# Grouped-query attention with a key/value cache: keys in rows of 32 KiB, two units to a K buffer, two V buffers

## The chip, the core and the metric

One core of a Trainium2 chip runs the kernel. The metric is the device time in microseconds (us), the median of the runs. The engines are named as in the profile: PE (matrix products; PEld its weight loads), DVE (vector), ACT (scalar), POOL (GpSimd) and SP, whose queue issues all of this kernel's transfers. Each engine takes its instructions in the order in which the program names them, and waits at one for the semaphores of its inputs and of the buffer that it writes.

## What is computed

```python
B, Sq, D = 8, 4, 512
Hq, Hkv, Sk, Dh = 32, 8, 2048, 128
rep = Hq // Hkv
q = (x @ wq).reshape(B, Sq, Hq, Dh).transpose(0, 2, 1, 3)
k = jnp.repeat(k_cache, rep, axis=1)
v = jnp.repeat(v_cache, rep, axis=1)
scores = jnp.einsum("bhqd,bhkd->bhqk", q, k) * (Dh ** -0.5)
p = softmax(scores, axis=-1)
o = jnp.einsum("bhqk,bhkd->bhqd", p, v)
out = o.transpose(0, 2, 1, 3).reshape(B, Sq, Hq * Dh) @ wo
```

All arrays are bf16. k_cache and v_cache have 33.6 MB each, wq and wo 4.2 MB each, x 32 KB.

## The kernel before

The work is cut into 16 **units**: a unit is one batch entry with four of the eight key heads (units 0 to 7 have heads 0 to 3, units 8 to 15 heads 4 to 7). Its K is 2 MB and its V is 2 MB. In memory the four heads of a batch entry lie one behind the other, so a unit's K is cut into 128 rows of 64 keys (16 KiB), one for each partition: 32 partitions a head. V is cut in the same way. K has a ring of three buffers (k_sb), V of three (the pool v_sb).

A unit goes through these steps.

- Turns (L143): DVE transposes blocks of 32 x 32 words of k_sb, half a unit at a time, into kt, which puts the key's elements on the partitions. kt has a ring of three.
- Scores (L218): eight matmuls for each turn, in four pairs. The weights are q_bd, the queries of four heads on a block diagonal. The two of a pair write the upper and the lower 64 partitions of s_ps and take different keys of kt. The first score set of a unit needs the first turn, the second the second.
- Maxima (L236, L228, L242): DVE takes the greatest score over both halves; its negative is less.
- Exponentials (L254): ACT reads s_ps, writes s_sb and sums into l_sb.
- Spread: POOL adds the two halves of the sums (L228, L287: "sums"); DVE turns s_sb into p_t (L264); ACT and POOL copy p_t in eight pieces, four each, into probs (L274); DVE inverts the sum (r_sb, L292). probs has two buffers.
- Values (L303): 32 matmuls in four quarters, with probs as weights and V as the moving operand, into o_ps.
- Divide (L323): ACT scales o_ps into o_sc. Finish (L340, L341): PE turns o_sc into o_t, DVE copies that into oT.

After eight units oT is turned to tokens (nat, L354) and to rows for wo (perm, L370); at the end out_ps is the product with wo (L385).

One loop over n names the work of several units: the sums of n - 1, both turns of n, the first score set of n, finish of n - 3, the second score set of n, the spread and r_sb of n - 1, maxima and exponentials of n, then values and divide of n - 2. The loads are named at the end of each turn of the loop by load_ready, from a list in the order K3, V1, K4, V2, ...: a K load as soon as the buffer's last turns are named, a V load as soon as its last values are. On SP they then stand in this order, and each waits until the engine has read the buffer. Ahead of the loop SP has K0, wq, x, K1 with K2, V0, K3, V1. wo uses wq's place, in six pieces behind V15.

x lies in a kt buffer at first. The queries come from it: PE turns x (xtp, L155), DVE copies (xT_sb, L162), PE multiplies with wq (psq, L169), ACT scales (q_nat, L180), DVE turns (q_t, L189) and POOL, DVE and ACT lay q_bd out (L195), for each half of the heads; the second half is made at n = 2 and 3.

Of the kernel before, what the change touches and what calls it, by code (L numbers as in the profile page):

```python
# [8 lines left out]
BF16 = mybir.dt.bfloat16  # L9
# [5 lines left out]
def kernel(  # L15
# [20 lines left out]
    C = Sk // S  # L36
    HQ = rep * Sq
    NQ = G * HQ
    NT, CT = 2, C // 2
    HP = 8  # L40
    WR = 8
    NP = Hq // HP
    DH = D // 2
    NU = (Hkv // G) * B
    KB, VB, PB, LAG = 3, 3, 2, 2
    XR = 8
    scale = float(Dh) ** -0.5
    AX = mybir.AxisListType.X
# [5 lines left out]
    align.tile([128, 192], BF16, name="pad")  # L54
    wpool = ctx.enter_context(tc.tile_pool(name="wpool", bufs=1))
    kpool = ctx.enter_context(tc.tile_pool(name="kpool", bufs=1))
    vpool = ctx.enter_context(tc.tile_pool(name="vpool", bufs=VB))
    ktpool = ctx.enter_context(tc.tile_pool(name="ktpool", bufs=3))
    const = ctx.enter_context(tc.tile_pool(name="const", bufs=1))
    small = ctx.enter_context(tc.tile_pool(name="small", bufs=2))  # L60
# [5 lines left out]
    order = ctx.enter_context(tc.manual_schedule())  # L66

    wq_sb = wpool.tile([128, R, HqDh], BF16, tag="w", name="wq_sb")
    x_sb = ktpool.tile([128, CT, 2, S, 2], BF16, tag="kt", name="x_sb")
    xT_sb = const.tile([128, R, T], BF16, name="xT_sb")  # L70
    q_bd = const.tile([128, Hkv // G, 2, 2, B, G, HQ], BF16, name="q_bd")
    probs = [const.tile([128, 2, C // 4, 2, G, HQ], BF16, name=f"probs{i}") for i in range(PB)]
# [9 lines left out]
    ks = [None] * NU
    vs = [None] * NU

    k_sb = kpool.tile([128, KB, C, Dh], BF16, name="k_sb")

    def load_k(u, n=1):
        hq, b = units[u]
        nc.sync.dma_start(
            k_sb[:, u % KB : u % KB + n, :, :].rearrange("p b c d -> p b (c d)"),  # L90
            k_cache[b : b + n, G * hq : G * hq + G].rearrange(
                "b g (s c) d -> (g s) b (c d)", c=C
            ),
        )
        for i in range(n):
            ks[u + i] = k_sb[:, (u + i) % KB, :, :]

    def load_v(u):
        hq, b = units[u]
        vs[u] = vpool.tile([128, C, Dh], BF16, tag="v_sb", name="v_sb")  # L100
        of = v_cache[b, G * hq : G * hq + G].rearrange("g (s c) d -> (g s) c d", c=C)
        nc.sync.dma_start(vs[u][:, :, :], of)

    def load_wo(p, r0, n):
        rows = wo[p * HP * 128 : (p + 1) * HP * 128, :].rearrange("(q r) j -> q r j", r=WR)
# [2 lines left out]

    load_k(0)
    nc.sync.dma_start(wq_sb[:, :, :], wq.rearrange("(p r) n -> p r n", r=R))  # L110
    x_all = x_sb[:T, :, :, :, :].rearrange("q c h s e -> q (c h s e)")
    nc.vector.memset(x_all, 0.0)  # L112
    nc.sync.dma_start(x_all[::XR, :], x.flatten_outer_dims().rearrange("(a i) d -> a (i d)", i=XR))
    load_k(1, 2)
    loads = [("v", 0)]
    for u in range(3, NU + 2):
        if u < NU:
            loads.append(("k", u))
        loads.append(("v", u - 2))
    loads.reverse()  # L120

    def load_ready(nk, nv):
        while loads:
            kind, u = loads[-1]
            if u >= (nk + KB if kind == "k" else nv + VB):
                return
            (load_k if kind == "k" else load_v)(u)
            loads.pop()

    load_ready(0, 0)  # L130

    make_identity(nc, ident[:])
    make_identity(nc, ident4[:])
# [4 lines left out]

    kts = {}

    def turn_keys(u, t):
        kts[(u, t)] = ktpool.tile([128, CT, 2, S, 2], BF16, tag="kt", name="kt")
        nc.vector.transpose(  # L143
            kts[(u, t)][:, :, :, :, :].rearrange("k c h s e -> k (c h s e)").bitcast(FP32),
            ks[u][:, t * CT : (t + 1) * CT, :].rearrange("s c d -> s (c d)").bitcast(FP32),
        )

    for t in range(NT):
        turn_keys(0, t)

    xtp = psum_m.tile([128, R, T], FP32, tag="m", name="xtp")
    for i in range(XR):
        row = x_all[:, i * D : (i + 1) * D].rearrange("q (p r) -> q r p", r=R)
        for r in range(R):
# [5 lines left out]
                stop=True,  # L160
            )
    nc.vector.tensor_copy(out=xT_sb[:, :, :], in_=xtp[:, :, :])  # L162

    def q_products(hq):
        psq = psum_m.tile([128, rep * Dh], FP32, tag="m", name="psq")
        for r in range(R):
            for g in range(G):
                c0 = (hq * G + g) * rep * Dh
                nc.tensor.matmul(  # L169
                    psq[g * T : (g + 1) * T, :],  # L170
                    lhsT=xT_sb[:, r, :],
                    rhs=wq_sb[:, r, c0 : c0 + rep * Dh],
                    start=(r == 0),
                    stop=(r == R - 1),
                )
        return psq
# [31 lines left out]
    s_pss = {}  # L208
    less = {}

    def scores(u, t):
        hq, b = units[u]
        if t == 0:
            s_pss[u] = psum_s.tile([128, NT, CT // 2, S], FP32, tag="s", name="s_ps")
        for i in range(4):
            k, e = i // 2, i % 2
            for h in range(2):
                nc.tensor.matmul(  # L218
                    s_pss[u][h * NQ : (h + 1) * NQ, t, :, :],
                    lhsT=q_bd[:, hq, k, e, b, :, :].rearrange("k g q -> k (g q)"),  # L220
                    rhs=kts[(u, t)][:, h * CT // 2 : (h + 1) * CT // 2, k, :, e],
                    start=(i == 0),
                    stop=(i == 3),
                )
# [7 lines left out]
    def maxima(u):  # L232
        top = small.tile([128, 1], FP32, tag="top", name="top")
        swapped = small.tile([128, 1], FP32, tag="swapped", name="swapped")
        less[u] = small.tile([128, 1], FP32, tag="less", name="less")
        nc.vector.reduce_max(  # L236
            out=top[:, :],
            in_=s_pss[u][:, :, :, :].rearrange("q t c s -> q (t c s)"),
            axis=AX,
        )  # L240
        swap_halves(nc.vector, swapped, top)
        nc.vector.tensor_scalar(  # L242
            out=less[u][:, :],
            in0=swapped[:, :],
            scalar1=top[:, 0:1],
            scalar2=-1.0,
            op0=mybir.AluOpType.max,
            op1=MULT,
        )

    def exponentials(u):
        s_sbs[u] = small.tile([128, C // 4, S, 2], BF16, tag="s_sb", name="s_sb")
        l_sbs[u] = totals.tile([128, 1], FP32, tag="l_sb", name="l_sb")
        nc.scalar.activation(  # L254
            out=s_sbs[u][:, :, :, :].rearrange("q a s j -> q a j s"),
            in_=s_pss[u][:, :, :, :].rearrange("q t (a j) s -> q (t a) j s", j=2),
            func=EXP,
            bias=less[u][:, 0:1],
            accum_out=l_sbs[u][:, :],
        )  # L260
# [22 lines left out]
    def sums(u):  # L283
        swapped = small.tile([128, 1], FP32, tag="l_swapped", name="l_swapped")
        total = small.tile([128, 1], FP32, tag="l_total", name="l_total")
        swap_halves(nc.gpsimd, swapped, l_sbs[u])
        nc.gpsimd.tensor_tensor(out=total[:, :], in0=l_sbs[u][:, :], in1=swapped[:, :], op=ADD)  # L287
        return total
# [8 lines left out]
    def values(u, quarter):  # L297
        if quarter == 0:
            o_pss[u] = psum_o.tile([128, 2, Dh], FP32, tag="o", name="o_ps")
        t, h = quarter // 2, quarter % 2  # L300
        for a in range(CT // 4):
            c = quarter * C // 4 + 2 * a
            nc.tensor.matmul(  # L303
                o_pss[u][:, :, :].rearrange("n j d -> n (j d)"),
                lhsT=probs[u % PB][:, h, t * CT // 4 + a, :, :, :].rearrange(
                    "s j g q -> s (j g q)"
                ),
                rhs=vs[u][:, c : c + 2, :].rearrange("s c d -> s (c d)"),
                start=(c == 0),
                stop=(c == C - 2),  # L310
            )
# [79 lines left out]
                )  # L391

    pieces = [(0, 0, 8), (1, 0, 8), (2, 0, 8), (3, 0, 5), (3, 5, 2), (3, 7, 1)]
    for n in range(NU + LAG):
        w = n - LAG
        if 0 < n <= NU:
            total = sums(n - 1)
        if 0 < n < NU:
            turn_keys(n, 0)
            turn_keys(n, 1)  # L400
        if n < NU:
            scores(n, 0)
        if w >= 1 and n < NU:
            finish(w - 1)
        if n < NU:
            scores(n, 1)
        if n == 2:
            q_ps = q_products(1)
        if n == 3:
            spread_q(1, q_nat, [by_gpsimd] * G)  # L410
        if 0 < n <= NU:
            probs_to_keys(n - 1)
            inverses(n - 1, total)
        if n < NU:
            maxima(n)
            exponentials(n)
        if n == 2:
            q_nat = scale_q(q_ps)
        if w == B + 1:
            to_tokens(0)  # L420
        if w == B + 2:
            to_wo_rows(0)
        if w >= 0:
            for quarter in range(4):
                values(w, quarter)
            if n >= NU:
                finish(w - 1)
            (divide_all if w == NU - 1 else divide)(w)
        load_ready(min(n + 1, NU), max(w + 1, 0))
        if n == NU - 1:  # L430
            assert not loads, loads
            for piece in pieces:
                load_wo(*piece)

    out_ps = [psum_s.tile([128, DH], FP32, tag="s", name="out_ps") for _ in range(2)]
    half = WR // 2
# [42 lines left out]
```

## Time and profile before

| what | value |
|---|---|
| median of 3 runs | 185.16 us (185.07 to 185.16) |
| the profiled execution | 185.0 us, span 183.1 us |
| PE / DVE / ACT / POOL busy | 123.2 / 121.2 / 77.9 / 59.3 us |
| granted PE clock, mean | 0.925 |
| read from memory | 75.53 MB, 413 GB/s over the span |
| DMA packets | 5666, 1044 of them under 8 KB |
| first wait for x | 18.7 us |
| scores wait for turns, in total | 34.6 us, 27 times |
| turns wait for K, in total | 17.8 us, 9 times |

The span is the time from the first to the last instruction; the time of a run has some 2 us around it. A group of the profile has line, engine, operation, output and input with their shapes, count, then busy time and mean ns of one, then the idle time of the engine before them and what ended most of it. A line of the timeline has start and length in us, engine, line, operation, and in brackets the idle time before it. The chain of waits is followed back from the last instruction: at each step to what released it.

### The profile page before, as it was taken

To read this page: it belongs to the slowest core of one execution; us is meant where nothing else is said; L and a number is where in the kernel's file an instruction comes from. 1 tells how busy PE (TensorE), PEld (TensorE's weight loads), DVE (VectorE), ACT (ScalarE), POOL (GpSimd) and SP (SyncE) were. 2 spreads that over 40 slices of the span, in tenths; PEclk is the share of its full clock that TensorE was granted. 3 is DMA by queue.
4 is the path that set the end of the run, shared out by engine and by line. 5 is a ranking of instruction groups with operands and counts; after the bars stand their busy time and mean duration, and the time that the engine had idled before them with its cause. 6 is when DMAs were issued, how large, how long until landed. Compare 5 with 4: busy or idle time off the path is not lost.

```text
span 183.1 us, 2559 instructions
## 1 busy us (share of the span) xinstructions
PE 123.2 (67%) x962; PEld 80.4 (44%) x962; DVE 121.2 (66%) x157; ACT 77.9 (43%) x136; POOL 59.3 (32%) x127
## 2 busy tenths in 40 slices
PE   0000652709997978869396878397776978399993
PEld 0000320303664736647154455256463656268872
DVE  6380027797989899894967768576948594946120
ACT  2000112264547748548154544529281719075030
POOL 8900020343237525415151514224240506056000
PEclk9999999995899999999969699969997599969999
DMA  6989999999999999999999999999999999999991
GB/s 182 497 386 419 426 433 429 433 433 426 429 429 437 429 431 420 438 419 437 426 433 429 433 426 437 422 437 433 426 433 429 429 433 426 433 426 422 426 392 49
DMA packets 5666, 75.70 MB, mean 413 GB/s; under 512 B 628, under 2 KB 788, under 8 KB 1044
## 3 DMA queue, kind: packets, MB, share of 16 engines
q1 hardware_dynamic: 5656, 75.57, 97.1%
q8 instruction: 7, 0.11, 0.2%
q14 instruction: 3, 0.02, 0.0%
HBM read 75.53 MB, written 0.03 MB: 413 GB/s over the span
## 4 chain that ended last, share of the span: by engine, by line
DMA 58%; DVE 23%; PE 13%; issue 1%; SPq 1%; POOL 1%; ACT 0%
DMA k_sb<-in_k_cache_dram 38%; DVE kt L143 17%; DMA wo_sb<-in_wo_dram 12%; DMA x_sb<-in_x_dram 8%; PE s_ps L218 6%; PE o_ps L303 4%; DVE top L236 3%; PE psq L169 2%; DVE x_sb L112 1%; SPq L107 1%; POOL q_bd L195 1%; DVE q_t L189 1%; PE out_ps L385 1%; DVE swapped L228 1%; PE xtp L155 1%
## 5 line engine op out<-in xcount | busy, mean ns | idle before, releaser
L143 DVE STREAM_TRANSPOSE kt<-k_sb 128x2048 f32<-128x2048 f32 x32 | 72.0, 2288 | 17.8 <-DMA k_sb<-in_k_cache_dram 17.8
L218 PE MATMUL s_ps<-kt,q_bd 128*64 128x512 bf16 x256 | 44.3, 477 | 37.5 <-DVE kt L143 34.6
L303 PE MATMUL o_ps<-v_sb,probs 128*128 128x256 bf16 x512 | 62.4, 284 | 0.3 <-ACT oT L341 0.3
L274 ACT COPY probs<-p_t 32x512 bf16<-32x512 bf16 x62 | 38.1, 615 | 52.8 <-DVE r_sb L292 51.7
L303 PEld LDWEIGHTS <-probs 128*128 128x128 bf16 x512 | 50.9, 102 | 15.1 <-issue 6.7
L274 POOL COPY probs<-p_t 32x512 bf16<-32x512 bf16 x63 | 38.6, 613 | 56.6 <-DVE r_sb L292 54.3
L218 PEld LDWEIGHTS <-q_bd 128*64 128x64 bf16 x256 | 16.9, 125 | 55.1 <-issue 24.7
L236 DVE TENSOR_REDUCE top<-s_ps 128x1 f32<-128x1024 f32 x16 | 19.6, 1223 | 16.0 <-PE s_ps L218 16.0
L254 ACT ACTIVATE s_sb<-s_ps,less 128x1024 bf16<-128x1024 f32 x16 | 22.4, 1399 | 10.6 <-DVE less L242 10.4
L228 POOL COPY l_swapped<-l_sb 64x1 f32<-64x1 f32 x32 | 5.8, 181 | 32.0 <-ACT s_sb L254 31.3
L155 PE MATMUL xtp<-ident,x_sb 32*128 32x4 bf16 x32 | 1.2, 169 | 18.7 <-DMA x_sb<-in_x_dram 18.7
L323 ACT ACTIVATE o_sc<-o_ps,r_sb 64x128 f32<-64x128 f32 x28 | 10.1, 362 | 7.5 <-PE o_ps L303 6.8
L264 DVE STREAM_TRANSPOSE p_t<-s_sb 128x512 f32<-128x512 f32 x16 | 11.0, 689 | 1.6 <-ACT s_sb L254 1.6
L195 POOL COPY q_bd<-q_t 32x512 bf16<-32x512 bf16 x6 | 3.8, 626 | 18.7 <-DVE q_t L189 18.6
L180 ACT ACTIVATE q_nat<-psq 128x512 bf16<-128x512 f32 x2 | 1.2, 590 | 20.2 <-PE psq L169 20.2
L155 PEld LDWEIGHTS <-x_sb 32*128 32x128 bf16 x32 | 1.1, 112 | 18.7 <-issue 18.7
L340 PEld LDWEIGHTS o_t<-both,o_sc 128*128 128x128 f32 x30 | 4.9, 205 | 6.1 <-issue 4.8
L136 POOL MEMSET probs<- 128x4096 bf16 x2 | 7.0, 3513 | 0.0
L340 PE MATMUL o_t<-both,o_sc 128*128 128x64 f32 x30 | 6.8, 312 | 0.0
L341 DVE CAST oT<-o_t 128x64 bf16<-128x64 f32 x14 | 2.7, 193 | 4.7 <-PE o_t L340 4.7
L228 DVE COPY swapped<-top 64x1 f32<-64x1 f32 x32 | 4.7, 148 | 0.8
L162 DVE CAST xT_sb<-xtp 128x128 bf16<-128x128 f32 x1 | 0.3, 291 | 7.0 <-PE xtp L155 7.0
(37 smaller groups left out, 46.0 us busy)
## 6 DMA issues: line engine op xcount, KB each, us to landing
v_sb<-in_v_cache_dram SPq DMA_DIRECT2D x16, 2048.0 KB, 23.3
k_sb<-in_k_cache_dram SPq DMA_DIRECT2D x14, 2048.0 KB, 23.5
wq_sb<-in_wq_dram SPq DMA_DIRECT2D x1, 4096.0 KB, 17.2
k_sb<-in_k_cache_dram SPq DMA_DIRECT2D x1, 4096.0 KB, 24.3
wo_sb<-in_wo_dram SPq DMA_DIRECT2D x3, 1024.0 KB, 18.9
wo_sb<-in_wo_dram SPq DMA_DIRECT2D x1, 640.0 KB, 21.9
wo_sb<-in_wo_dram SPq DMA_DIRECT2D x1, 256.0 KB, 22.0
wo_sb<-in_wo_dram SPq DMA_DIRECT2D x1, 128.0 KB, 19.6
```

The lines of the kernel that those rows point to most:

```text
L136: nc.gpsimd.memset(pr[:, :, :, :, :, :], 0.0)
L143: nc.vector.transpose(kts[(u, t)][:, :, :, :, :].rearrange("k c h s e -> k (c h s e)").bitcast(FP32), ks[u][:, t * CT : (t + 1) * CT, :].r ...
L195: engines[g](out=q_bd[rows, hq, :, :, :, g, :].rearrange("w k e b (h s) -> w (k e b) h s", h=rep), in_=q_t[rows, :, :, :, :].rearrange("w ...
L218: nc.tensor.matmul(s_pss[u][h * NQ : (h + 1) * NQ, t, :, :], lhsT=q_bd[:, hq, k, e, b, :, :].rearrange("k g q -> k (g q)"), rhs=kts[(u, t) ...
L228: engine.tensor_copy(out=out[h * NQ : (h + 1) * NQ, :], in_=in_[(1 - h) * NQ : (2 - h) * NQ, :])
L236: nc.vector.reduce_max(out=top[:, :], in_=s_pss[u][:, :, :, :].rearrange("q t c s -> q (t c s)"), axis=AX,)
L254: nc.scalar.activation(out=s_sbs[u][:, :, :, :].rearrange("q a s j -> q a j s"), in_=s_pss[u][:, :, :, :].rearrange("q t (a j) s -> q (t a ...
L264: nc.vector.transpose(p_t[:, :, :, :, :].rearrange("s x g q j -> s (x g q j)").bitcast(FP32), s_sbs[u][:, :, :, :].rearrange("q a s j -> q ...
L274: by[h * G + g](out=probs[u % PB][g * S : (g + 1) * S, h, :, :, g, :], in_=p_t[quad * S : (quad + 1) * S, :, g % 2, :, :].rearrange("s x q ...
L303: nc.tensor.matmul(o_pss[u][:, :, :].rearrange("n j d -> n (j d)"), lhsT=probs[u % PB][:, h, t * CT // 4 + a, :, :, :].rearrange("s j g q ...
L323: nc.scalar.mul(out=to, in_=of, mul=by)
L340: nc.tensor.matmul(o_t[:, :], lhsT=o_scs[u][:, :], rhs=both[:, :], start=True, stop=True)
```

## The change

K is loaded by pairs of units: 2p and 2p + 1, two batch entries with the same heads. A unit's K is now cut into 64 rows of 128 keys (32 KiB); the first unit of the pair lies in the even partitions and the second in the odd ones, by two transfers of 2 MB. There are two such buffers (64 KiB a partition, where three of 16 KiB were 48) and two V buffers (32 KiB, where three were 48). V of units 13 and 14 goes into the K buffer that pair 6 leaves. x lies in the first V buffer until it is read, and V0 and V1 come as one transfer behind that.

A pair has four turns of the old size, and each brings keys of both units: eight matmuls for each, where the pair of matmuls that run together are now of two units and read every second block column of kt. s_ps of a unit has its two halves of keys in other places, exp reads them from two runs of PSUM by turns, and values takes the halves of probs in another order.

The loop runs over pairs p. Per turn it names: turn 0, its scores, finish of unit 2p - 3; turn 1, its scores; two quarters of values of 2p - 2; turn 2, its scores, a quarter; turn 3, its scores, a quarter, divide; maxima and exponentials of 2p and of 2p + 1; finish of 2p - 2; the spread of 2p; values and divide of 2p - 1; the spread of 2p + 1; then V(2p), V(2p + 1) and K of pair p + 2 on SP. The last two pairs have another order, and the values of units 13 to 15 follow the loop.

```diff
-    NT, CT = 2, C // 2
+    NT, CT = 4, C // 2
+    CP = 2 * C
+    SH = S // 2
...
-    KB, VB, PB, LAG = 3, 3, 2, 2
+    KB, VB, PB, LAG = 2, 2, 2, 2
+    NPAIR = NU // 2
...
+    k_sb = kpool.tile([128, KB, CP, Dh], BF16, name="k_sb")
+    v_sb = vpool.tile([128, VB, C, Dh], BF16, name="v_sb")
+    spare = k_sb[:, NPAIR % KB, :, :]
+    vs = [v_sb[:, u % VB, :, :] for u in range(NU)]
+    for i, u in enumerate((NU - 3, NU - 2)):
+        vs[u] = spare[:, i * C : (i + 1) * C, :]
+
+    def load_k(p):
+        hq, b = units[2 * p]
+        for i in range(2):
+            nc.sync.dma_start(
+                k_sb[i::2, p % KB, :, :],
+                k_cache[b + i, G * hq : G * hq + G].rearrange("g (s c) d -> (g s) c d", c=CP),
+            )
...
     load_k(0)
     nc.sync.dma_start(wq_sb[:, :, :], wq.rearrange("(p r) n -> p r n", r=R))
...
-    load_k(1, 2)
...
+    load_k(1)
...
-    for t in range(NT):
+    for t in range(3):
         turn_keys(0, t)
...
     nc.vector.tensor_copy(out=xT_sb[:, :, :], in_=xtp[:, :, :])
+    load_v(0, 2)
...
+        turned = kts[(p, t)][:, :, :, :, :].rearrange("k c w (s b) e -> k c w b s e", b=2)
         for i in range(4):
             k, e = i // 2, i % 2
-            for h in range(2):
+            for j, u in enumerate(pair):
+                hq, b = units[u]
+                h = (t + j) % 2
                 nc.tensor.matmul(
-                    s_pss[u][h * NQ : (h + 1) * NQ, t, :, :],
+                    s_pss[u][h * NQ : (h + 1) * NQ, t // 2, :, :],
                     lhsT=q_bd[:, hq, k, e, b, :, :].rearrange("k g q -> k (g q)"),
-                    rhs=kts[(u, t)][:, h * CT // 2 : (h + 1) * CT // 2, k, :, e],
+                    rhs=turned[:, :, k, j, :, e],
...
-            in_=s_pss[u][:, :, :, :].rearrange("q t (a j) s -> q (t a) j s", j=2),
+            in_=s_pss[u][:, :, :, :].rearrange("q i c s -> q c s i"),
...
+    def spread(u):
+        total = sums(u)
+        probs_to_keys(u)
+        inverses(u, total)
+
+    def softmax_top(u):
+        maxima(u)
+        exponentials(u)
...
+    done = None
+    for p in range(NPAIR):
+        last = p == NPAIR - 1
+        one, two = (2 * p - 2, 2 * p - 1) if p else (None, None)
+        if p == NPAIR - 2:
+            two = None
+        if last:
+            one, two = 2 * p - 3, 2 * p - 2
+        for t in range(2):
+            if p:
+                turn_keys(p, t)
+            scores(p, t)
+            if t == 0 and done is not None:
+                finish(done)
+        if p == 1:
+            q_nat = scale_q(q_products(1))
+        if p == 2:
             spread_q(1, q_nat, [by_gpsimd] * G)
...
+        quarters(one, 0, 1)
+        if p:
+            turn_keys(p, 2)
+        scores(p, 2)
+        quarters(one, 2)
+        turn_keys(p, 3)
+        if p == 0:
+            load_k(KB)
+        scores(p, 3)
+        quarters(one, 3)
+        if one is not None:
+            divide(one)
+        softmax_top(2 * p)
+        if last:
+            spread(NU - 3)
+        softmax_top(2 * p + 1)
+        if one is not None:
+            finish(one)
+        if last:
+            quarters(two, 0, 1, 2, 3)
+            divide(two)
+            spread(2 * p)
+        else:
+            spread(2 * p)
+            quarters(two, 0, 1, 2, 3)
+            if two is not None:
+                divide(two)
+            if p != NPAIR - 2:
+                spread(2 * p + 1)
+        done = two
+        if p and p < NPAIR - 2:
+            load_v(2 * p)
+            if p < NPAIR - 3:
+                load_v(2 * p + 1)
+            load_k(p + 2)
+        elif p == NPAIR - 2:
+            load_v(NU - 5)
+            for u in (NU - 4, NU - 3, NU - 2):
+                load_v(u)
+        elif last:
+            load_v(NU - 1)
             for piece in pieces:
                 load_wo(*piece)
+    for w in range(NU - 3, NU):
+        quarters(w, 0, 1, 2, 3)
+        finish(w - 1)
+        (divide_all if w == NU - 1 else divide)(w)
+        if w == NU - 3:
+            spread(NU - 1)
```

More of the change, by code (lines that the diff above doesn't have):

```diff
@@ L56 @@
     kpool = ctx.enter_context(tc.tile_pool(name="kpool", bufs=1))
-    vpool = ctx.enter_context(tc.tile_pool(name="vpool", bufs=VB))
+    vpool = ctx.enter_context(tc.tile_pool(name="vpool", bufs=1))
     ktpool = ctx.enter_context(tc.tile_pool(name="ktpool", bufs=3))
@@ L68 @@
     wq_sb = wpool.tile([128, R, HqDh], BF16, tag="w", name="wq_sb")
-    x_sb = ktpool.tile([128, CT, 2, S, 2], BF16, tag="kt", name="x_sb")
     xT_sb = const.tile([128, R, T], BF16, name="xT_sb")
@@ L81, with load_v @@
     units = [(hq, b) for hq in range(Hkv // G) for b in range(B)]
[L82 to L87, printed above, removed]
+    k_sb = kpool.tile([128, KB, CP, Dh], BF16, name="k_sb")
[11 more added lines that the diff above has]
+            )
+    def load_v(u, n=1):
         hq, b = units[u]
+        to = v_sb[:, u % VB : u % VB + n, :, :] if n > 1 else vs[u].rearrange("p (n c) d -> p n c d", n=1)
         nc.sync.dma_start(
-            k_sb[:, u % KB : u % KB + n, :, :].rearrange("p b c d -> p b (c d)"),
-            k_cache[b : b + n, G * hq : G * hq + G].rearrange(
+            to.rearrange("p b c d -> p b (c d)"),
+            v_cache[b : b + n, G * hq : G * hq + G].rearrange(
                 "b g (s c) d -> (g s) b (c d)", c=C
@@ L94, in load_k @@
         )
[L95 to L102, printed above, removed]
     def load_wo(p, r0, n):
@@ L110 @@
     nc.sync.dma_start(wq_sb[:, :, :], wq.rearrange("(p r) n -> p r n", r=R))
-    x_all = x_sb[:T, :, :, :, :].rearrange("q c h s e -> q (c h s e)")
+    x_all = v_sb[:T, 0, :, :].rearrange("q c d -> q (c d)")[:, : XR * D]
     nc.vector.memset(x_all, 0.0)
     nc.sync.dma_start(x_all[::XR, :], x.flatten_outer_dims().rearrange("(a i) d -> a (i d)", i=XR))
-    load_k(1, 2)
[L115 to L130, printed above, removed]
+    load_k(1)
     make_identity(nc, ident[:])
@@ L139, with turn_keys @@
     kts = {}
-    def turn_keys(u, t):
-        kts[(u, t)] = ktpool.tile([128, CT, 2, S, 2], BF16, tag="kt", name="kt")
+    def turn_keys(p, t):
+        kts[(p, t)] = ktpool.tile([128, CT, 2, S, 2], BF16, tag="kt", name="kt")
         nc.vector.transpose(
-            kts[(u, t)][:, :, :, :, :].rearrange("k c h s e -> k (c h s e)").bitcast(FP32),
-            ks[u][:, t * CT : (t + 1) * CT, :].rearrange("s c d -> s (c d)").bitcast(FP32),
+            kts[(p, t)][:, :, :, :, :].rearrange("k c h s e -> k (c h s e)").bitcast(FP32),
+            k_sb[:, p % KB, t * CT : (t + 1) * CT, :].rearrange("s c d -> s (c d)").bitcast(FP32),
         )
-    for t in range(NT):
+    for t in range(3):
         turn_keys(0, t)
@@ L209, with scores @@
     less = {}
-    def scores(u, t):
-        hq, b = units[u]
+    def scores(p, t):
+        pair = (2 * p, 2 * p + 1)
         if t == 0:
-            s_pss[u] = psum_s.tile([128, NT, CT // 2, S], FP32, tag="s", name="s_ps")
+            for u in pair:
+                s_pss[u] = psum_s.tile([128, 2, CT, SH], FP32, tag="s", name="s_ps")
+        turned = kts[(p, t)][:, :, :, :, :].rearrange("k c w (s b) e -> k c w b s e", b=2)
         for i in range(4):
             k, e = i // 2, i % 2
-            for h in range(2):
+            for j, u in enumerate(pair):
+                hq, b = units[u]
+                h = (t + j) % 2
                 nc.tensor.matmul(
-                    s_pss[u][h * NQ : (h + 1) * NQ, t, :, :],
+                    s_pss[u][h * NQ : (h + 1) * NQ, t // 2, :, :],
                     lhsT=q_bd[:, hq, k, e, b, :, :].rearrange("k g q -> k (g q)"),
-                    rhs=kts[(u, t)][:, h * CT // 2 : (h + 1) * CT // 2, k, :, e],
+                    rhs=turned[:, :, k, j, :, e],
                     start=(i == 0),
@@ L237, in maxima @@
             out=top[:, :],
-            in_=s_pss[u][:, :, :, :].rearrange("q t c s -> q (t c s)"),
+            in_=s_pss[u][:, :, :, :].rearrange("q i c s -> q (i c s)"),
             axis=AX,
@@ L254, in exponentials @@
         nc.scalar.activation(
-            out=s_sbs[u][:, :, :, :].rearrange("q a s j -> q a j s"),
-            in_=s_pss[u][:, :, :, :].rearrange("q t (a j) s -> q (t a) j s", j=2),
+            out=s_sbs[u][:, :, :, :].rearrange("q a w j -> q a j w"),
+            in_=s_pss[u][:, :, :, :].rearrange("q i c s -> q c s i"),
             func=EXP,
@@ L299, in values @@
             o_pss[u] = psum_o.tile([128, 2, Dh], FP32, tag="o", name="o_ps")
-        t, h = quarter // 2, quarter % 2
-        for a in range(CT // 4):
+        h, a0 = (quarter // 2 + u) % 2, quarter % 2 * (C // 8)
+        for a in range(C // 8):
             c = quarter * C // 4 + 2 * a
@@ L304, in values @@
                 o_pss[u][:, :, :].rearrange("n j d -> n (j d)"),
-                lhsT=probs[u % PB][:, h, t * CT // 4 + a, :, :, :].rearrange(
+                lhsT=probs[u % PB][:, h, a0 + a, :, :, :].rearrange(
                     "s j g q -> s (j g q)"
@@ L393 @@
     pieces = [(0, 0, 8), (1, 0, 8), (2, 0, 8), (3, 0, 5), (3, 5, 2), (3, 7, 1)]
[L394 to L409, printed above, removed]
-            spread_q(1, q_nat, [by_gpsimd] * G)
[L411 to L419, printed above, removed]
+    def spread(u):
+        total = sums(u)
+        probs_to_keys(u)
+        inverses(u, total)
@@ new lines, in softmax_top, with quarters @@
+    def softmax_top(u):
+        maxima(u)
+        exponentials(u)
+    def quarters(u, *which):
+        if u is not None:
+            for quarter in which:
+                values(u, quarter)
+    done = None
[15 more added lines that the diff above has]
+        if p == 2:
+            spread_q(1, q_nat, [by_gpsimd] * G)
+        if p == B // 2 + 1:
@@ L420 @@
             to_tokens(0)
-        if w == B + 2:
+        if p == B // 2 + 2:
             to_wo_rows(0)
[L423 to L431, printed above, removed]
+        quarters(one, 0, 1)
+        if p:
+            turn_keys(p, 2)
+        scores(p, 2)
```

## The prediction

> **What bounds it now.** I read the page's head, the slices and the queues first. Columns of the third line: packets, MB, share of the time of 16 engines.
>
> ```profile
> span 183.1 us, 2559 instructions
> ...
> DMA  6989999999999999999999999999999999999991
> ...
> q1 hardware_dynamic: 5656, 75.57, 97.1%
> ...
> DMA 58%; DVE 23%; PE 13%; issue 1%; SPq 1%; POOL 1%; ACT 0%
> ```
>
> The DMA engines are busy from the second slice to the 39th; 75.5 MB at the 430 GB/s of the windows between 40 and 155 us is 175.6 us of a 183.1 us span. After the last wo piece (178.99 in the chain of waits) only 4.1 us follow. So anything that leaves the queue empty is paid in full, and anything that makes the engines' work between transfers longer than the transfers becomes the bound instead. How much room is there? The groups with their mean ns:
>
> ```profile
> L143 DVE STREAM_TRANSPOSE kt<-k_sb 128x2048 f32<-128x2048 f32 x32 | 72.0, 2288 | 17.8 <-DMA k_sb<-in_k_cache_dram 17.8
> L218 PE MATMUL s_ps<-kt,q_bd 128*64 128x512 bf16 x256 | 44.3, 477 | 37.5 <-DVE kt L143 34.6
> L303 PE MATMUL o_ps<-v_sb,probs 128*128 128x256 bf16 x512 | 62.4, 284 | 0.3 <-ACT oT L341 0.3
> ...
> L274 POOL COPY probs<-p_t 32x512 bf16<-32x512 bf16 x63 | 38.6, 613 | 56.6 <-DVE r_sb L292 54.3
> ```
>
> DVE has 7.0 us a unit (two turns 4.54, maxima 1.71 start to start, p_t 0.61, oT and r_sb 0.2) and PE 6.14 in an undisturbed 9.75 us window. Between 55 and 75 us, where K was there ahead, units follow each other every 7.4 us: before's order keeps DVE always supplied, since p_t of the last unit and oT stand between its turns and its maxima, and cover PE's second score set. The queue's own timeline and the chain tell how deep the cover is: a K load lands 24 us after its issue, five transfers are out at once. The chain also gives the start:
>
> ```profile
> 3.01 15.56 DMA x_sb<-in_x_dram
> ...
> 25.09 3.64 PE s_ps L218 x16
> ```
>
> x queues behind K0 (2 MB) and wq, lands at 18.57; scores start 6.5 us later.
>
> **The change, part by part.** Times are on the profile's scale; s1, s2 ... is where DVE begins turn 0 of pair 1, 2 ...
>
> Wider rows. The trace's packet records have 611 ns for a 16 KiB packet and 1213 for each of wq's 128 of 32 KiB. K's 2048 packets become 1024: 1024 x 9 ns / 16 engines = 0.58 us less transfer. That is all that can be gained. The count of transfers stays 40, and halves of 2 MB cost nothing extra: the present ones of 2 MB run at a DMA share of 1.01.
>
> The start. K0 is now 4 MB ahead of wq and x: 2.1 MB at 430 GB/s is 4.87 us, x lands at 23.4, scores start at 29.9. Four cold sets (3.63 us for two in the row above) end at 37.0; two maxima 3.4; exp of unit 1 ends at 42.1, but r_sb(1) waits on POOL, whose four copies of unit 0 (2.56) and sums(1) (0.67) come after p_t(0) (41.1): 44.4. s1 = 44.5, where before has already turned three units.
>
> The queue. Issued by then: K0, wq, K1, V0-V1, K2, 21 MB, which ends at 18.57 + 14.7 MB / 431 = 52.6. The next issue, V2, waits for all of values(0), and V3 and K3 stand behind it on SP, though K3's buffer is free earlier (turn 3 of pair 1). values(0) is spread among the score sets of pair 1 and ends at s1 + 13.4 = 57.9 at best. With 1.5 us from issue to data (the row of out_dram) DMA idles 6.8 us. No cover is left: two V buffers instead of three.
>
> The loop. Offsets from the first turn, PE at its best pace (8 score matmuls 1.10, 32 of values 3.67): turn 0 to 2.27; scores 0 to 3.40; o_t and oT of the previous unit stand before turn 1 in DVE's order, to 3.95; turns 1 to 3 end at 6.22, 8.49, 10.76. PE: scores 1 to 7.35, two quarters to 9.15, scores 2 to 10.2, a quarter to 11.1, scores 3 to 12.2. Only then DVE's maxima (it has nothing left to do): 12.23 to 15.65; oT, p_t to 16.45; POOL's four copies to 19.12 and sums of the second unit to 19.79; r_sb of that unit at 19.85, and behind it the next turn at **19.95**. DVE's waits in it: 1.5 for oT, 1.5 for scores 3, 0.8 for the second exp, 1.8 for POOL. Transfers per pair: 256 packets of V x 611 ns / 16 = 9.78, 128 of K x 1213 / 16 = 9.70, in sum 19.48. So the engines, not DMA, set the pace by half a microsecond, and every us more on this chain counts. Pair 1 takes 20.3 (no oT wait, but 1.9 of psq), pair 2 20.4 (q_t), pair 5 20.65 (nat transposes), pair 6, without the second spread and with perm, 17.25.
>
> The end. Pair 7 from its first turn: scores 3 end at 10.6, values(12) 16.4; ACT, in order, does exp(14), copies(13) to 16.6, exp(15), divide(12), copies(14) to 21.5; values(14) follow to 25.2, values(15) with an o_t between to 29.3. Before, values(15) end at 173.87 and the span 9.2 later, 0.25 of it a wait for wo: 38.3. V15 and wo, issued at 11.5, need 1.5 + 14.6 us and hold nothing up.
>
> Sum at best pace: 44.5 + 20.3 + 20.4 + 20 + 20 + 20.65 + 17.25 + 38.3 = 201.4.
>
> PE's clock. PE would idle 4.2 us between values and the next turn's scores, and 2.4 more before scores 1. What such gaps do:
>
> ```profile
> 89.81 1.13 PE L218 MATMUL s_ps<-kt,q_bd 128*64 128x512 bf16 x8 [2.87 <-DVE kt L143]
> ...
> 92.00 1.92 PE L218 MATMUL s_ps<-kt,q_bd 128*64 128x512 bf16 x8 [0.69 <-DVE kt L143]
> 93.85 4.21 PE L303 MATMUL o_ps<-v_sb,probs 128*128 128x256 bf16 x32
> ...
> 109.25 1.06 PE L218 MATMUL s_ps<-kt,q_bd 128*64 128x512 bf16 x8 [1.29 <-DVE kt L143]
> ...
> 119.04 1.92 PE L218 MATMUL s_ps<-kt,q_bd 128*64 128x512 bf16 x8 [2.89 <-DVE kt L143]
> ```
>
> All four gaps over 2.2 us after 80 us were followed by a stretch at half pace, and cost 1.3, 1.4, 2.9 and 1.3 us of PE time (mean 1.7); gaps of 1.3 and 1.7 cost nothing. In the new loop this time lies on the chain. Ends: 0, and 3.4 (both score sets and two quarters at half pace: 0.8 + 0.3 + 0.8 + 1.5). I take 1.7, the rows' mean, for seven pairs: 11.9. Span 213.3. The profiled run took 185.0 us for its span of 183.1, so 1.9 lies around it; 185.0 is 0.16 under the median of 185.16. **215 us.**
>
> [...]
>
> Costs that no row shows. The score matmuls read with a step of 8 bytes instead of 4: nothing at the low end (x_sb's weight loads have that step, 112 ns against 102 of probs), half as much again at the high (nat_sb's with 16 bytes: 165), 7 x 4 x 0.55 = 15 us; I take 0, the row with the same step. exp reads two PSUM runs 2 KiB apart by turns: 0 (q_nat, step 8 bytes: 590 ns against 573 for a plain 512 copy) to twice 1.40, which passes through POOL's copies as 1.2 a pair, 8.4 in all; I take 0. [...] Turns, p_t, probs, values keep shape and price; other indices alone cost nothing.
>
> **Rivals.** 1: the loop overlaps better than my order says, so that DMA stays the bound after its one idle stretch: 179.0 + 6.8 - 0.6 + 4.1 + 1.9 = 191. For it: only 0.5 us separates the two paces; against it: PE's gaps, and each wait follows from an engine's order. 2: PE at half pace through both score sets and two quarters in every pair: 201.4 + 7 x 3.4 + 1.9 = 227. For it: gaps longer than any above; against it: one of four gaps cost over 1.4. 3, the other side: V2 is issued before the queue runs dry, by 51.1, transfers stay back to back and the wide rows pay: 185.0 - 0.6 = 184.4. It decides on values(0) ending 7 us sooner than reckoned; for it, before never starved; against it, x lands 4.87 later, and SP's order is fixed. [...]
>
> **Numbers.** Forecast 0.70 (its own range 203 to 222, clock cost 0 to 2.7), rival 1 0.08, rival 2 0.12, rival 3 0.05, rival 4 0.05. The range holds the forecast and rival 2: 199 to 228. A change within 0.2% is about what a measurement can't tell from none: faster 0.03, same 0.02 (both rival 3), slower 0.95.
>
> **What would show it.** DMA slices with a hole near 53 to 60 us and about a tenth idle after; the 32 KiB packets in the count (some 1,020 fewer); turn 0 starts 20 to 23 us apart; DVE's waits put down to oT, scores 3 and POOL's sums; scores at 1.1 or 1.9; kt's turns never waiting for k_sb after pair 1. Wrong if turns wait for K, if the pace is 19.5 with full DMA slices, if exp is above 1.4 us or score sets at full clock above 1.1.

## The result, and the profile after

| kernel | median, us | runs | ratio to before, 95% interval |
|---|---|---|---|
| before | 185.16 (185.07 to 185.19) | 6 | |
| after | 324.78 (323.69 to 325.93) | 6 | 1.7537 (1.7497 to 1.7577) |

The forecast was 215, its range 199 to 228. The direction was right and the size was not: 139.6 us were lost where 30 were forecast. The page of the changed kernel, in the order in which before was read (head, slices, queue, the chain's shares by engine, groups):

```profile
span 322.7 us, 2556 instructions
...
DMA  7999917502992019940089600797006980198990
...
q1 hardware_dynamic: 4632, 75.57, 57.3%
...
DMA 41%; PE 38%; DVE 16%; SPq 2%; ACT 1%; issue 1%; POOL 0%; DVEq 0%; ACTq 0%
...
L212 PE MATMUL s_ps<-kt,q_bd 128*64 128x512 bf16 x256 | 61.8, 620 | 136.4 <-DVE kt L132 133.5
L132 DVE STREAM_TRANSPOSE kt<-k_sb 128x2048 f32<-128x2048 f32 x32 | 71.8, 2285 | 113.6 <-DMA k_sb<-in_k_cache_dram 110.5
...
L297 PE MATMUL o_ps<-v_sb,probs 128*128 128x256 bf16 x448 | 54.8, 277 | 0.0
...
L268 POOL COPY probs<-p_t 32x512 bf16<-32x512 bf16 x63 | 38.5, 612 | 18.0 <-DVE r_sb L286 13.6
```

The same 75.57 MB are moved in 1,024 packets fewer, and the turns, the values and POOL's copies have their old durations (2285 ns, 277, 612). Two things are new. The DMA slices have not one hole, as forecast, but seven, and the turns wait 110.5 us for K, where before they waited 17.8: DMA stands idle, and yet the engines wait for DMA. And a score matmul takes 620 ns where it took 477. The middle of the chain of waits shows the first at work (start, us, what):

```profile
102.16 2.32 DVE kt L132
...
121.12 3.51 PE o_ps L297 x32
125.60 18.42 DMA k_sb<-in_k_cache_dram
144.05 2.32 DVE kt L132
```

SP's queue in the same pair (start, us, line, what is issued):

```profile
119.83 5.15 SPq L102 DMA_DIRECT2D v_sb<-in_v_cache_dram  x2
125.07 1.12 SPq L94 DMA_DIRECT2D k_sb<-in_k_cache_dram  x2
```

Pair 2's turns start at 102.16. The two V loads at 119.83 are V4 and V5, and the K load at 125.07 is K4: the program names K2 within pair 0 and K(p + 2) at the end of pair p. The turn that starts at 144.05 when this load has landed is pair 3's, and pair 3 uses K3, which was issued at 82.67 and whose landing released pair 2's first turn at 102.16. So each pair's first turn waits for the **next pair's K**. The start says it most plainly: K0 is in at 13.3 us, and the very first turn starts at 33.20, when K1 is in. What one pair costs then stands in series: 22.9 us from the first turn to the issue of K, and 19.0 from there until it is in, 41.9 together, where the forecast had 22.1 for this pair (20.4 and 1.7 for the clock).

The compiled program says the same. This is what DVE's first turn of pair 0 and that of pair 1 wait for, by the semaphores of the loads, in the changed kernel, and then in the same kernel with its K buffers as two tiles (two_tiles, below):

```
L132 StreamTranspose kt<-k_sb 128x2048 [waits DMAHW4_49,DMAHW5_49,DMAHW1_49,DMAHW0_49]
L132 StreamTranspose kt<-k_sb 128x2048 [waits DMAHW7_49,DMAHW0_49]

L132 StreamTranspose kt<-k_sb0 128x2048 [waits DMAHW1_49,DMAHW0_49]
L132 StreamTranspose kt<-k_sb1 128x2048 [waits DMAHW5_49,DMAHW4_49]
```

Four semaphores are two loads of two transfers each: K0's are 1 and 0, K1's 4 and 5. In the changed kernel pair 0 waits for both loads, and pair 1 for 7 and 0, which are K2's.

### The profile page after: what moved, and what is told of

Read it like the earlier page. It is cut to its first block, busy times and chain, and to the rows that moved or that the text cites. A ratio compares the mean times of both kernels' runs of the same rounds, so it can differ in the third digit from the quotient of the medians.

```text
span 322.7 us, 2556 instructions
## 1 busy us (share of the span) xinstructions
PE 138.0 (43%) x962; PEld 77.8 (24%) x962; DVE 122.7 (38%) x157; ACT 77.3 (24%) x136; POOL 59.2 (18%) x127
## 3 DMA queue, kind: packets, MB, share of 16 engines
q1 hardware_dynamic: 4632, 75.57, 57.3%
## 4 chain that ended last, share of the span: by engine, by line
DMA 41%; PE 38%; DVE 16%; SPq 2%; ACT 1%; issue 1%; POOL 0%; DVEq 0%; ACTq 0%
DMA k_sb<-in_k_cache_dram 41%; PE o_ps L297 17%; PE s_ps L212 16%; DVE kt L132 13%; PE o_t L334 2%; SPq L94 1%; PE out_ps L379 1%; ACT o_sc L317 1%; DVE top L230 1%; PE psq L159 1%; DVE v_sb L117 1%; POOL q_bd L185 0%; SPq L102 0%; PE perm L364 0%; DVE oT L335 0%
## 5 line engine op out<-in xcount | busy, mean ns | idle before, releaser
L212 PE MATMUL s_ps<-kt,q_bd 128*64 128x512 bf16 x256 | 61.8, 620 | 136.4 <-DVE kt L132 133.5
L132 DVE STREAM_TRANSPOSE kt<-k_sb 128x2048 f32<-128x2048 f32 x32 | 71.8, 2285 | 113.6 <-DMA k_sb<-in_k_cache_dram 110.5
L297 PE MATMUL o_ps<-v_sb,probs 128*128 128x256 bf16 x448 | 54.8, 277 | 0.0
L297 PEld LDWEIGHTS <-probs 128*128 128x128 bf16 x512 | 49.0, 100 | 22.3 <-issue 16.0
L230 DVE TENSOR_REDUCE top<-s_ps 128x1 f32<-128x1024 f32 x16 | 19.5, 1219 | 35.4 <-PE s_ps L212 35.4
L248 ACT ACTIVATE s_sb<-s_ps,less 128x1024 bf16<-128x1024 f32 x16 | 22.4, 1398 | 13.2 <-DVE less L236 12.7
L144 PE MATMUL xtp<-ident,v_sb 32*128 32x4 bf16 x32 | 1.2, 169 | 23.8 <-DMA v_sb<-in_x_dram 23.8
L335 DVE CAST oT<-o_t 128x64 bf16<-128x64 f32 x14 | 3.1, 220 | 20.4 <-PE o_t L334 20.4
L334 PE MATMUL o_t<-both,o_sc 128*128 128x64 f32 x30 | 7.5, 339 | 6.2 <-ACT o_sc L317 6.2
L159 PE MATMUL psq<-wq_sb,xT_sb 128*32 128x512 bf16 x32 | 2.9, 505 | 15.3 <-DVE xT_sb L151 15.3
L353 ACT COPY nat_sb<-nat 64x512 bf16<-64x512 bf16 x3 | 1.6, 578 | 24.4 <-PE nat L348 24.4
L297 PE MATMUL o_ps<-k_sb,probs 128*128 128x256 bf16 x64 | 7.3, 273 | 0.1
L286 DVE RECIPROCAL r_sb<-l_total 128x1 f32<-128x1 f32 x16 | 2.5, 157 | 12.5 <-POOL l_total L281 12.5
```

The costliest lines, as they stand in the source:

```text
L132: nc.vector.transpose(kts[(p, t)][:, :, :, :, :].rearrange("k c h s e -> k (c h s e)").bitcast(FP32), k_sb[:, p % KB, t * CT : (t + 1) * C ...
L159: nc.tensor.matmul(psq[g * T : (g + 1) * T, :], lhsT=xT_sb[:, r, :], rhs=wq_sb[:, r, c0 : c0 + rep * Dh], start=(r == 0), stop=(r == R - 1),)
L212: nc.tensor.matmul(s_pss[u][h * NQ : (h + 1) * NQ, t // 2, :, :], lhsT=q_bd[:, hq, k, e, b, :, :].rearrange("k g q -> k (g q)"), rhs=turne ...
L230: nc.vector.reduce_max(out=top[:, :], in_=s_pss[u][:, :, :, :].rearrange("q i c s -> q (i c s)"), axis=AX,)
L248: nc.scalar.activation(out=s_sbs[u][:, :, :, :].rearrange("q a w j -> q a j w"), in_=s_pss[u][:, :, :, :].rearrange("q i c s -> q c s i"), ...
L297: nc.tensor.matmul(o_pss[u][:, :, :].rearrange("n j d -> n (j d)"), lhsT=probs[u % PB][:, h, a0 + a, :, :, :].rearrange("s j g q -> s (j g q)"
```

## The experiments

**A false wait.** The theory: writing `k_sb[i::2, p % KB, :, :]`, every other partition of one buffer of a tile that holds both, is tracked as touching both buffers, so a turn waits for whatever load was named last. Rivals: the alternate partitions move slowly, or the queue's order alone starves the turns. Two kernels take the changed one; in two_tiles each buffer is a tile of its own, in halves the tile stays and a unit lies in 64 neighbouring partitions.

```diff
-    k_sb = kpool.tile([128, KB, CP, Dh], BF16, name="k_sb")
+    k_sb = [kpool.tile([128, CP, Dh], BF16, name=f"k_sb{i}") for i in range(KB)]
...
-                k_sb[i::2, p % KB, :, :],
+                k_sb[p % KB][i::2, :, :],
```

> The changed kernel with its two K buffers as two separate tiles; nothing else. Theory A (a turn waits for the transfer of the next pair's K, because a transfer into every other partition of one tile is taken to touch both of its buffers): the 18 to 28 us that DVE waits for k_sb in each pair go away, the pace falls from 41.9 us a pair to 20 to 22, and the time comes to what the order of the loop alone gives, 205 to 222 us. Theory B (the order of the loop and the two V buffers cost the time, and the waits for K are only where it shows): 300 us or more. Theory C (transfers into every other partition land late in themselves): 300 us or more.

228.62 us (226.96 to 229.67), ratio 1.2329 (1.2266 to 1.2393). What DVE waited for (us in total, times, longest):

```profile
DVE top L230 <- PE s_ps L212: 38.5, 8, 6.0
DVE oT L335 <- PE o_t L334: 20.4, 7, 3.6
DVE r_sb L286 <- POOL l_total L281: 12.4, 7, 2.0
DVE kt L132 <- DMA k_sb<-in_k_cache_dram: 8.6, 1, 8.6
```

The turns' wait for K goes from 110.5 us to 8.6, once, at the start, and the time falls by 96.2. No transfer, instruction or order was changed. What is left on DVE is what the forecast had listed: oT, the scores, POOL's sums.

```diff
-                k_sb[i::2, p % KB, :, :],
+                k_sb[64 * i : 64 * i + 64, p % KB, :, :],
```

> The changed kernel with one K tile as it is, but the two units of a pair loaded into partitions 0 to 63 and 64 to 127 instead of even and odd ones; the scores then mix the two units' keys and the output is left wrong by that, the work is the same. Theory A: no step, so no wait for the other buffer, 205 to 222 us as with two tiles, unless a transfer into 64 neighbouring partitions runs at another rate than one into 64 alternate ones (packets of 32 KiB over 1213 ns; at half rate 262 us or more). Theory B: 300 us or more.

286.73 us in one run. Here, too, the compiled first turn waits for its own two transfers alone; in the trace it starts at 23.75 us, when K0 is in (22.8 by the packet records) and K1 is not (53.0). So it is the step over partitions, not the shared tile by itself, that widens the wait. But another cost takes its place (second slice line: GB/s):

```profile
DMA  8899999999989999999989998999999999984990
GB/s 184 189 216 368 373 207 189 304 403 221 221 216 435 234 214 196 386 299 221 210 257 410 214 212 193 375 279 214 203 318 193 219 191 371 414 343 147 418 368 14
```

The engines of DMA are busy throughout, at some 215 GB/s whenever K moves. By the packet records a 32 KiB packet of K takes 2564 ns (the median of 1024) where it took 1213 in the changed kernel, as wq's did before: here a transfer into 64 neighbouring partitions runs at about half the rate of one into every other partition.

The same wait was then put into the kernel before: each unit's K by two transfers into every other partition, first in its one tile of three buffers (before_step), then in three tiles (before_step_tiles).

```diff
+            rows = k_cache[b + i, G * hq : G * hq + G].rearrange("g (s c) d -> (g s) (c d)", c=C)
+            for j in range(2):
+                nc.sync.dma_start(
+                    k_sb[j::2, (u + i) % KB, :, :].rearrange("p c d -> p (c d)"), rows[j::2, :]
+                )
...
# before_step_tiles
-    k_sb = kpool.tile([128, KB, C, Dh], BF16, name="k_sb")
+    k_sb = [kpool.tile([128, C, Dh], BF16, name=f"k_sb{i}") for i in range(KB)]
```

> The kernel before, whose only edit is that each unit's K comes by two transfers, into the even and the odd partitions, in the same one tile. Theory A: each unit's turns wait for the K load issued last, three units ahead, instead of their own; a K load then lands some 10 to 12 us after its issue and a unit takes 14 to 17 us instead of 9.75: 240 to 290 us. Theory B: 184 to 188 us.

> The same as before_step but with the three K buffers as three tiles. Theory A: back at 184 to 188 us, since the transfers themselves are as fast. Theory C: well above, 200 us or more.

240.75 us in one run, against 185.32 in three tiles (185.13 to 185.69; ratio 1.0017, 1.0008 to 1.0027). The turns' group in the one tile, then in three:

```profile
L142 DVE STREAM_TRANSPOSE kt<-k_sb 128x2048 f32<-128x2048 f32 x32 | 72.0, 2289 | 75.8 <-DMA k_sb<-in_k_cache_dram 75.8
```

```profile
L142 DVE STREAM_TRANSPOSE kt<-k_sb 128x2048 f32<-128x2048 f32 x32 | 72.0, 2288 | 18.4 <-DMA k_sb<-in_k_cache_dram 18.4
```

The two differ in nothing but the tiles: the wait costs 55.4 us even in a kernel with nothing of pairs or wide rows, while the transfers into alternate partitions, and twice as many of them, cost by themselves 0.17%, 0.3 us.

**The read step.** In two_tiles a score set took 1.9 to 2.0 us everywhere, also beside values at full pace (PE, start and us):

```profile
104.71 1.98 PE L212 MATMUL s_ps<-kt,q_bd 128*64 128x512 bf16 x8
106.62 1.05 PE L297 MATMUL o_ps<-v_sb,probs 128*128 128x256 bf16 x8
107.59 1.90 PE L212 MATMUL s_ps<-kt,q_bd 128*64 128x512 bf16 x8
109.43 1.05 PE L297 MATMUL o_ps<-v_sb,probs 128*128 128x256 bf16 x8
```

So this is not the clock: eight matmuls of values between two such sets take 1.05, and the granted clock from 104.7 to 110 us is 1.00. Theory: the 8-byte step of the moving operand. It was put alone into the kernel before (before_read8: every second block column, the keys in another order than the values'), then with both matmuls of a pair on the same columns (read8_same).

```diff
-                    rhs=kts[(u, t)][:, h * CT // 2 : (h + 1) * CT // 2, k, :, e],
+                    rhs=kts[(u, t)][:, :, k, h::2, e],
...
+                    rhs=kts[(u, t)][:, :, k, 0::2, e],
```

> The kernel before with one edit: the two matmuls of a pair read every second block column of kt (a step of 8 bytes) instead of the upper and lower half of it (4 bytes); the keys then come in another order than the values, which the output does not follow. Theory D: score sets of 1.9 us also beside values at full pace, where they were 1.10; the time stays within 184 to 188 us, since PE has 6.1 us of work in 9.75 and DMA is the bound. Theory E: sets stay at 1.1.

> The kernel before, whose score matmuls read every second block of columns of one half with an 8-byte step, and both units of a pair the same columns: the keys of one half are used twice and the other half's not at all. If the step alone makes a set of eight cost 1.9 us (theory: the read step), the sets stay at 1.90 us as in before_read8. If it was that two concurrent streams read different halves of the same bytes (rival), they come back to 1.05 to 1.15 us. The time is set by the transfers in both: 184 to 188.

185.28 and 185.11 us, one run each. The score matmuls (ns min/median/max) in before, before_read8 and read8_same:

```profile
L218 PE MATMUL s_ps<-kt,q_bd x256: 376/402/637, 25.1 to 161.4; 128*64 128x512 bf16 x128
```

```profile
L218 PE MATMUL s_ps<-kt,q_bd x256: 589/609/662, 25.0 to 162.0; 128*64 128x512 bf16 x128
```

```profile
L218 PE MATMUL s_ps<-kt,q_bd x256: 588/609/661, 25.0 to 161.4; 128*64 128x512 bf16 x128
```

The set is slow whichever columns the other matmul reads, and the least duration is 588 ns: there is no full pace left to fall from. These edits also read runs of 16 columns where before reads runs of 32; turn_apart below reads runs of 16 with a 4-byte step, for two units at once as two_tiles does, and has sets of 1.05, so neither the shorter runs nor the second unit is the cause, but the step. In the kernel before it costs no time, as DMA sets the end there. With the 8-byte step a set takes 1.90 us instead of 1.06 to 1.10. That holds for two matmuls that run together (in the kernel before the two of a pair start at most 59 ns apart and take 376 ns or more each); no run here has one alone.

What the step is worth in the loop: two_tiles, with the scores reading as before (two_tiles_step4).

```diff
-                    rhs=turned[:, :, k, j, :, e],
+                    rhs=kts[(p, t)][:, j * CT // 2 : (j + 1) * CT // 2, k, :, e],
```

> The version with two K tiles (228.62), whose score matmuls read with the 4-byte step of the kernel before: a unit takes one half of the blocks of columns in place of its own rows of keys, so units' keys are mixed; the turns, their duration and every other instruction stay. This is the loop that the prediction reckoned with: turns that wait for their own K alone, score sets of 1.1 us at full clock. Theory (false wait plus read step explain the miss): sets come down from 1.9 to 1.05 to 1.1 where PE runs at full clock, which is 4 x 0.85 = 3.4 us of each pair, over seven pairs 23.8, and the time is 203 to 209, up to 215 (the figure on record) where the idle time that opens on PE brings sets at half pace back, as the prediction had it. Rival (something else in the loop is slow, the sets were hidden): the time stays at 224 to 230.

218.24 us (217.55 to 219.55), ratio 1.1817 (1.1776 to 1.1859): 10.4 less, not 20 to 26, and a miss, as even the upper end was 215. PE in one pair:

```profile
89.74 1.92 PE L212 MATMUL s_ps<-kt,q_bd 128*64 128x512 bf16 x8 [4.54 <-ACT probs L268]
...
94.81 1.92 PE L212 MATMUL s_ps<-kt,q_bd 128*64 128x512 bf16 x8 [2.53 <-DVE kt L132]
...
99.71 1.06 PE L212 MATMUL s_ps<-kt,q_bd 128*64 128x512 bf16 x8
...
101.68 1.06 PE L212 MATMUL s_ps<-kt,q_bd 128*64 128x512 bf16 x8
```

The first two sets of a pair stand behind gaps of 4.54 and 2.53 us and run at half pace whatever their step (1.92 us here with 4 bytes, 1.96 and 1.93 in two_tiles with 8; granted clock 0.50 from 89.7 to 96.7 us); only the last two are at full pace (1.00 from 99.7 on), and 2 x 0.84 x 7 = 11.8 is about what came back. The expectation had counted four, and gave half pace only as its upper end.

**Buying the step back in the turn.** turn_apart: DVE writes the columns of even and odd partitions apart, so that the scores read with 4 bytes.

```diff
-        kts[(p, t)] = ktpool.tile([128, CT, 2, S, 2], BF16, tag="kt", name="kt")
+        kts[(p, t)] = ktpool.tile([128, CT, 2, 2, SH, 2], BF16, tag="kt", name="kt")
...
-            kts[(p, t)][:, :, :, :, :].rearrange("k c h s e -> k (c h s e)").bitcast(FP32),
+            kts[(p, t)][:, :, :, :, :, :].rearrange("k c h b s e -> k (c h b s e)").bitcast(FP32).rearrange("k (c b s) -> k c s b", b=2, s=SH),
...
-        turned = kts[(p, t)][:, :, :, :, :].rearrange("k c w (s b) e -> k c w b s e", b=2)
+        turned = kts[(p, t)]
```

> two_tiles, with the turns writing the even and the odd columns of each block of 32 to two places, so that a unit's keys lie side by side and the score matmuls read with a step of 4 bytes again instead of 8. Theory D (the step of 8 bytes holds a score set at 1.9 to 2.0 us even where the values beside it run at full pace): sets of 1.1 us at full pace, the pace falls from 24.5 us a pair by some 3, 205 to 213 us. Theory E (the sets are long because the two matmuls that run together now belong to two units, with other weights and other PSUM banks): sets stay at 1.9, 226 to 231 us. A turn's 2.29 us may grow by its scattered writes; that would show in its row.

240.63 us (240.0 to 241.77), ratio 1.3018 (1.2976 to 1.306): a miss. The last two sets of a pair did come down, to 1.05 (the first two stand behind gaps of 5.8 and 3.8 us), but the turn took this instead of 2285 ns:

```profile
L132 DVE STREAM_TRANSPOSE kt<-k_sb 128x2048 f32<-128x2048 f32 x32 | 113.1, 3610 | 11.5 <-DMA k_sb<-in_k_cache_dram 8.3
```

Four turns a pair at 1.3 us more are 5.3, against 1.7 won on PE.

**The order.** order2 takes two_tiles, names finish behind the second turn and the sums of both units ahead of the copies, so that oT and r_sb do not hold the turns; apart_order2 adds the scattered turn to it.

```diff
+        if p:
+            turn_keys(p, 0)
+            turn_keys(p, 1)
+        scores(p, 0)
+        if done is not None:
+            finish(done)
+        scores(p, 1)
...
+            totals_of = [sums(2 * p + i) for i in range(1 if p == NPAIR - 2 else 2)]
+            spread(2 * p, totals_of[0])
```

> two_tiles with another order on DVE and POOL: finish of the last unit after turn 1 instead of between turns 0 and 1, and the sums of both units ahead of the copies of the first. If these two waits of DVE (2.8 and 1.9 us a pair in two_tiles) lie on the chain as the prediction had it, the pace falls from 24.5 to about 20.7 us and the time to 207 to 213 us; if PE or ACT hold the loop, 224 to 230 us.

> turn_apart and order2 together. By the chain: 24.5 - 3 - 3.8 = some 17.5 us a pair, under the 19.5 us of the transfers, so that DMA is the bound again but for one idle stretch at the start, ahead of V2: 189 to 197 us. If the two do not add up because something else holds the loop: over 200 us.

order2 took 203.81 us (202.98 to 205.04), ratio 1.1014 (1.0968 to 1.1059), 24.8 less than two_tiles and below the range expected: DVE's wait for POOL is gone, that for oT is 0.3 to 0.6 us a pair instead of 2.75, and a pair takes 19.6 to 20.2 us instead of some 24.5. apart_order2 took 215.24 (213.4 to 215.84), ratio 1.1609 (1.1554 to 1.1663): the dear turn (3617 ns, the median) makes DVE the bound (in the pair from 87.31 to 108.75 us it waits 2.1), again a miss.

**Can the idea win?** pairs3 goes on from order2: x and wq ahead of K0, all four score sets ahead of a pair's values, and on SP K(p + 2) as soon as the last turn frees its buffer, ahead of the V loads. pairs4 moves three loads more.

```diff
-    load_k(0)
     nc.sync.dma_start(wq_sb[:, :, :], wq.rearrange("(p r) n -> p r n", r=R))
...
+    load_k(0)
     load_k(1)
...
         turn_keys(p, 3)
+        if p + 2 < NPAIR:
+            load_k(p + 2)
         scores(p, 3)
...
-            load_k(p + 2)
...
# pairs4
-        if p + 2 < NPAIR:
+        if p + 2 < NPAIR - 1:
             load_k(p + 2)
...
+            if p + 2 == NPAIR - 1:
+                load_k(p + 2)
...
-            for u in range(2 * p, NU):
+            for u in (NU - 3, NU - 2, NU - 4, NU - 1):
```

> The change rebuilt by what the runs showed, nothing left out: two tiles for K; wq and x ahead of K0; on DVE both first turns ahead of the finishes of the last two units; on PE all four score sets of a pair ahead of the values, so that DVE comes to its maxima sooner; the sums of both units ahead of the copies; on SP K of pair p + 2 as soon as turn 3 frees it, then V(2p) and V(2p + 1); the last two pairs like the others. By the chain a pair takes 17.5 us of the engines against 19.5 us of transfers, and no issue waits past the end of the queue: DMA is the bound throughout, 184 to 187 us, at best 0.6 us under the kernel before by the wider packets. If holes stay in the DMA slices or the sets of 1.9 us still hold the loop: 190 to 200 us.

> The version pairs3 (190.57) with two moves at its end: V13 and V14 are issued ahead of V12, and K7 behind V10 and V11, so that no load with a free buffer waits behind one without. If the small hole of 145 to 151 us came from that order, it closes (about 3.5 us by the page's slices of 7 and 9 tenths), the last V lands near 176 in place of 179, and the time is 186 to 188. If TensorE's own work after V11 (27.7 us, of which 3.4 us a pair by the score sets of 1.9 us) sets the end anyway, only 1 us or so is saved: 189 to 190.5. In either case it is not below the kernel before, since the 8-byte read step stays.

pairs3: 190.57 us (189.18 to 191.6, 6 runs), ratio 1.0289 (1.0248 to 1.0329). pairs4: 197.65 (196.59 to 198.56), ratio 1.0685 (1.0648 to 1.0722). Their slices:

```profile
DMA  6999999999999999999999999999999779999970
```

```profile
DMA  6999999999999999999999999969999999999500
```

pairs3 is nearly bound by DMA again; what it lacks are two slices of 7, from 146 to 155 us, and the last values, which end at 179.2 where before has 173.87; what each of the two costs was not separated. pairs4 missed: K7, now issued at 135.87 instead of 123.70, lands late, a turn waits 3.85 us for it, and the hole has only moved, to 126 us. No version here beats the kernel before. The 0.58 us that the wide rows could win do not show either: q1's share of the span is 94.9% of 188.0, 178.4 us, in pairs3 and 97.1% of 183.1, 177.8, before.

## Why the prediction was wrong

**The step that failed** is "The loop", with its premise in "The start" and "The queue" that a turn waits for its own pair's K alone: "r_sb of that unit at 19.85, and behind it the next turn at 19.95". K's new transfers were costed as transfers, for rate and count; what a wait on them covers, once they write every other partition of a tile with two buffers, was not asked. In the runs each next turn stood behind the other pair's load, 96.2 us (324.78 - 228.62) of the 109.8 by which the forecast was short; of the rest the read step below is 10.4 and everything else 3.2. "Wrong if turns wait for K" was on record as the sign, but no rival had that mechanism.

**A mis-sized term**: the 8-byte read step, taken at 0 with an upper end of 0.55 us a set. It is 0.84 (1.90 - 1.06). The row chosen, x_sb's weight loads, is that of another operand; the moving operand had no row. In the loop it cost 10.4 us (228.62 - 218.24), since half of the sets ran at half pace anyway (1.92 us each). Its sign, "score sets at full clock above 1.1", was on record too.

**The rest of the sum** is tested by two_tiles_step4, which is the loop that the prediction reckoned with: 218.24 against 215.0.

| step | on record | two_tiles_step4 |
|---|---|---|
| s1 | 44.5 | 43.70 |
| V2 issued | 57.9 | 57.58 |
| wait for oT, a pair | 1.5 | 2.73 |
| wait for scores 3, pairs 2 to 5 | 1.5 | 2.5 to 4.5 |
| the clock's cost, a pair, passed on in these two waits | 1.7 | 2.4 to 3.2 |
| wait for second exp, for POOL | 0.8, 1.8 | 0.77, 1.95 |
| pair 1 | 22.0 | 20.8 |
| pairs 2 to 5, each | 21.7 to 22.4 | 22.8 to 24.2 |
| pair 6 | 19.0 | 20.4 |
| from pair 7's first turn to the end | 38.3 + 1.7 | 36.7 |

The waits were the right ones, but the clock's term was too small: 1.7, the mean of four rows, where its upper end of 3.4 was nearer. In pairs 2 to 5 both first score sets ran at half pace (0.86 us each), and the two quarters of values behind them took 2.6 to 3.4 us where 1.92 is full pace: 2.4 to 3.2 in all. oT's wait was 1.2 us short because o_t stands behind the first of these sets. Pairs 2 to 6 together took 7.5 us more than forecast, and s1, pair 1 and the end 5.3 less, so that 218.24 stands so near 215.0 is partly luck.

Of the two gaps in two_tiles_step4, that of 4.54 us has a clock of 0.50 behind it; that of 2.53 comes while the clock is still at 0.50 and tests nothing. In the kernel before the clock fell to 0.50 behind the prediction's four gaps (2.87, 2.89, 2.26 and 2.76 us). The prediction left one out: 1.43 us ahead of the set at 99.49, after which the next set took 1.82 and the values 4.53 (granted clock 0.73 from 101.7 to 108 us). The gap of 1.72 ahead of the set at 128.73 cost nothing (granted clock 1.00 from 123 to 139 us), so these rows give no least gap behind which the clock falls.

**Right at 0**: exp from two runs of PSUM, 1398 ns against 1399; other indices of turns (2285 ns against 2288), values (277 against 284) and, within 16 ns, p_t (705 against 689).

**The rivals.** 4, K's transfers at half rate, falls: in the changed kernel K's 32 KiB packets into alternate partitions took 1213 ns (median), the figure that the forecast has for them; 2564 was measured in halves, into neighbouring ones. 1 and 3 fall with the false wait and also without it: in two_tiles_step4 V2 is issued at 57.58, where 3 needed 51.1, and pairs 2 to 5 take 22.8 us or more, where 1 needed the transfers' 19.5. pairs3, at 190.57, is near the 191 of rival 1 in another order than the change has. The mechanism of 2 was nearer than the forecast's own term (2.4 to 3.2 us a pair of its 3.4), but the shorter start, pair 1 and end kept the time at 218.24; that its 227 is near two_tiles, where the read step adds to the clock, is chance.

## What to carry to other kernels

When a transfer's destination changes its shape, ask not only what it moves but which waits the compiler derives from it: here idle DMA together with engines that wait for DMA was the mark of a wait for the wrong load, and a tile for each buffer removed it. Price an operand's step by a row of the same operand, and test a layout's read step alone in a kernel whose end it can't reach, where it shows in the durations undisturbed. A packing that can win 0.58 us by its packets must not put 0.84 us on each of 32 score sets, nor take the buffers that keep the queue full.

## What was not expected of the hardware

- With an 8-byte step of its moving operand, in bf16, a score matmul took 588 ns or more (median 609 in before_read8 and in read8_same, where both matmuls of a pair read the same bytes), with a 4-byte step 376 or more (median 402, before).
- DVE's 32 x 32 transpose of 128 x 2048 words took 3610 ns (mean, turn_apart) when successive words of its output go by turns to two runs that lie 16 words apart, and 2285 (after) when they are written in a row.
- 32 KiB packets into 64 neighbouring partitions took 2564 ns (median, halves), into every other partition 1213 (after).
